# A transformer block on one Trainium2 core: two tiles of x turned by DMA rather than by TensorE, and low parts computed amid the attention steps

## The chip, the core and the metric

The kernel runs on one core of one Trainium2 chip. The metric is the time of one execution in device microseconds; lower is better. Matrix products run on TensorE (PE in the profile), elementwise work on VectorE (DVE), ScalarE (ACT) and GpSimd (POOL), and nearly all DMAs are issued from the queue of SyncE (SP), which issues them in the order of the program.

## What is computed

One layer for S = 2048 rows of D = 512, with 32 heads of 16: a layer norm without weights, a product with wqkv, attention of each row to itself and seven earlier rows at a distance of 2, a product with wo, the residual; then a second norm, a product with w1 (512 x 1792), a squared ReLU, a product with w2, and the residual. Cut to what matters:

```python
q, k, v = (layernorm(x) @ wqkv) as 3 x 32 heads x 2048 x 16
idx = s - [0, 2, .. 14]
logits = (q[s] . k[idx]) / 4, masked where idx < 0
o = softmax(logits) weighted v[idx]
h = x + o @ wo
out = h + relu(layernorm(h) @ w1 + b1) ** 2 @ w2 + b2
```

## The kernel before

The 2048 rows are 16 tiles of 128 rows (rows a stride apart, so that the rows a window reaches lie in the same partition). All operands are f32. A product is made as three products of split operands: each operand is rounded to a **high part** (`xh`, `oh`: a ScalarE copy, L147, `hi`) and a **low part**, the rest (`xl`, `ol`: a VectorE subtraction, L150, `lo`), and `mm3` (L222) adds high x high, low x high and high x low, four matmuls each. The left operand has to be turned (rows to columns) first: `transposes` (L202) does it by four TensorE matmuls with the identity (L205) into a PSUM bank, from which the two parts are read.

A second way to turn is there for tiles of o (the attention's output) and of h: `turn_split` (L591) copies the tile on ScalarE into two planes of 16 bits (L594), `turn_dma` (L596) turns all eight 128x128 blocks of the planes by one DMA in SP's queue (L598), `turn_join` (L601) puts the halves together again on ScalarE (L603), and the high and low part follow as above. It uses no TensorE.

**Order of the work.** The program is written as a row of slots, one for each product or half product of TensorE. `end_slot(pe)` closes one: it runs the chores due (`at`), then `pump()`, then the late chores (`after`). `pump` (L417) issues attention steps: each is an operation of VectorE (the product of q and k, L343; sums over the head, L377; the mask, L386; maximum and difference, L394 and L396; the sum, L366, and its reciprocal; the weights, L371; the product with v, L354), with the exponential on ScalarE (L400) and sums on GpSimd (L411). It issues as many steps as keep a model clock of VectorE (`now["dve"]`) level with that of TensorE (`now["pe"]`).

**The stages.** In the first 16 slots (n = 0 to 15, loop at L951) TensorE makes q, k and v of tiles 0 to 3 by four groups of head pairs, `qkv(t, gp)` with t = n % 4. Then `first_phase(t0)` (L980) for t0 = 4, 6, ... 14 makes those of two tiles at a time, in twelve half products. Each result is copied out of its bank by ScalarE (`evac`, L501) into one of two halves of the buffer `y2`, in turn, and once a pair of tiles is there, `store` issues the DMAs (L480, L483) to `qkv_d` in DRAM. Four PSUM banks go round, so a product needs the evacuation of the product four before it, and an evacuation needs the store that last read its half of `y2`. `store_halo` (L470) copies a piece of what was stored, and so waits for that store. Attention loads k, q and v windows back (L251 for k and v, L264 for q); q is copied to PSUM by ScalarE (L272). Later come the products with wo (`wo_product`, L658; `h_add`, L637, adds the residual and starts the statistics of h) and the two products of the MLP.

For tiles 4 and 5 of x, the statistics (`x_stats`) are due in slots 8 and 9, the norm (L200) in slots 11 and 12, and `x_T` in slots 13 and 14: TensorE turns the tile, ScalarE makes the high part in that slot, VectorE the low part behind that slot's attention steps. The first product that needs tile 4 is the one behind slot 15. Tiles 6 and 7 are normed in half products 6 and 7 of `first_phase(4)` and turned in half products 9 and 11.

Of the kernel before, what the change touches and what calls it, by code (L numbers as in the profile page):

```python
# [9 lines left out]
F32R = mybir.dt.float32r  # L10
# [6 lines left out]
P = 128  # L17
KB = D // P
FB = F // P
R = 4  # L20
RI = 2
# [7 lines left out]
NEG = -4.0e9  # L29
ROWS = 15  # L30
LAG = 3
AS = (4, 5, 8, 9, 12, 13)
OV = (4, 5, 8, 9, 12, 13)
HV = (4, 5, 8, 9, 12, 13)
SLOW = 1.01, 1.10, 1.06
DELAY = 3
WJ = 2
# [1 line left out]
OT = 4, 5, 10, 12  # L39
WO = 7, 9, 13, 15  # L40
HT = 20, 20, 21, 23
OK = (-6, -2, 4), (-5, -1, 5), (3, 6, 10), (4, 7, 12)
HK = (12, 15, 18), (14, 16, 19)
W2 = (18,)
LH = 3, 4, 10, 11
OP = 6, 7, 12, 13
# [12 lines left out]
def block_kernel(ctx, tc, x, wqkv, wo, w1, b1, w2, b2, out):  # L59
# [42 lines left out]
    def row(name, shape=(P, D), dt=F32):  # L102
        return work.tile(list(shape), dt, name=name, tag="row", bufs=ROWS)
# [3 lines left out]

    due = {}
    late = {}
    now = {"slot": 0, "pe": 0.0, "dve": 0.0, "sub": -1}  # L110

    def at(delta, fn, *a):
        due.setdefault(now["slot"] + delta, []).append((fn, a))

    def after(delta, fn, *a):
        late.setdefault(now["slot"] + delta, []).append((fn, a))

    def end_slot(pe):
        now["pe"] += pe
        run(due)  # L120
        pump()
        run(late)
        now["slot"] += 1

    def run(chores):
        todo = chores.get(now["slot"], [])
        while todo:
            fn, a = todo.pop(0)
            fn(*a)
# [83 lines left out]
    def hi_T(tr, h_dst):  # L213
        for d, src in parts(tr, h_dst):
            hi(d, src)
# [201 lines left out]
    def pump(until=None):  # L417

        while (done[until] < G) if until is not None else (now["dve"] < now["pe"]):
            todo = sums[:]  # L420
            sums.clear()
            t = next(stream, "end")
            for a in todo:
                add_up(*a)
            if t == "end":
                now["dve"] = 1e9
                return
            if t is None:
                now["dve"] = max(now["dve"], now["pe"])
                return  # L430
            dve(t * SLOW[min(now['sub'] + 1, 2)])


    xt, xT = {}, {}
# [16 lines left out]
    def x_T(t):  # L451
        tr = transposes(xt.pop(t))
        xT[t] = row("xh", (P, KB, P), F32R), row("xl", (P, KB, P), F32R)
        at(0, hi_T, tr, [xT[t][0]])
        after(0, lo_T, tr, [xT[t][0]], [xT[t][1]])
# [104 lines left out]
    oT = {}  # L560
# [9 lines left out]
    def o_T(t):  # L570
        s, j = divmod(t, RI)
        pump(until=s)
        tr = transposes(o_t[s][:, j, :])
        if t % R == RI:

            ohl = att.tile([P, 2, KB, P], F32R, name="ohl", tag="o", bufs=3)
            oT[t] = ohl[:, 0], ohl[:, 1]
        else:
            oT[t] = row("oh", (P, KB, P), F32R), row("ol", (P, KB, P), F32R)
        at(0, hi_T, tr, [oT[t][0]])  # L580
        at(0, lo_T, tr, [oT[t][0]], [oT[t][1]])

    planes = {}
# [7 lines left out]
    def turn_split(key, src):  # L591

        planes[key] = src, row("pl")
        nc.scalar.copy(two_planes(planes[key][1]), halves_of(src))  # L594

    def turn_dma(key):  # L596
        src, pl = planes[key]
        nc.sync.dma_start_transpose(  # L598
            src.bitcast(U16).rearrange("p (n c) -> p n c", c=P), pl.bitcast(U16))

    def turn_join(key):  # L601
        src, pl = planes[key]
        nc.scalar.copy(halves_of(pl).rearrange("p two n -> p n two"),  # L603
                       two_planes(src).rearrange("p two n -> p n two"))
        planes[key] = pl.rearrange("p (k c) -> p k c", k=KB)
# [6 lines left out]
    def o_join(t):  # L612
        turn_join(("o", t))
        tr = planes.pop(("o", t))
        if t % R == RI:
            ohl = att.tile([P, 2, KB, P], F32R, name="ohl", tag="o", bufs=3)
            oT[t] = ohl[:, 0], ohl[:, 1]
        else:
            oT[t] = row("oh", (P, KB, P), F32R), row("ol", (P, KB, P), F32R)
        hi_T(tr, [oT[t][0]])  # L620
        after(0, lo_T, tr, [oT[t][0]], [oT[t][1]])

    def h_split(t):
        turn_split(("h", t), hn.pop(t))
# [12 lines left out]
    def h_add(t, ps):  # L637
        h = hs[t]
        nc.vector.tensor_tensor(out=h, in0=ps, in1=h, op=ALU.add)
        dve(0.7)  # L640
        (act_stats if t in AS else norm_stats)(t, h)

    def h_norm(t):
        hn[t] = row("hn")
# [306 lines left out]
    for n in range(16):  # L951
        gp, t = divmod(n, 4)
        qkv(t, gp, (lambda: start_T(t + 1)) if n < 3 else None)
        if n < 2:
            x_norm(n + 2)
        if n == 0:
            x_stats(3)
        if n < 6:
            for k in (0, 1):
                at(0, hi_wqkv, n // 2 + 1, n % 2 * 2 + k)  # L960
                after(0, lo_wqkv, n // 2 + 1, n % 2 * 2 + k,
                      nc.gpsimd if k or n < 2 else nc.vector)
        if n == 1:
            load_wqkv(3)
        if n == 13:
            consts()
        if n in (5, 6, 12, 14):
            at(0, load_x, n - 1 if n < 7 else n // 2)
        if n in (8, 9):
            at(0, x_stats, n - 4)  # L970
        if n in (11, 12):
            at(0, x_norm, n - 7)
        if n in (13, 14):
            x_T(n - 9)
        end_slot(2.09)


# [2 lines left out]
    def first_phase(t0):  # L980
        def chores(m):
            if t0 + 3 < 16:
                if m in (0, 2):
                    at(0, x_stats, t0 + 2 + m // 2)

                early = t0 == 12
                if m + early in (6, 7):
                    at(0, x_norm, t0 - 4 + m + early)
                if m in XT[early]:
                    x_T(t0 + 2 + XT[early].index(m))  # L990
            if t0 + 5 < 16 and m in (6, 9):
                at(0, load_x, t0 + 2 + m // 3)
            if jobs and m % 3 == 0:
                at(0, weight_job)
            k = t0 // 2 * 12 - 72 + m
            if k == 19:
                dve(HOLD)
            for t in range(R):
                if k == OT[t]:
                    at(0, load_h, t)  # L1000
                    if t not in OV:
                        o_T(t)
                if t in OV and k in OK[t]:
                    at(0, (o_split, lambda t: turn_dma(("o", t)), o_join)[OK[t].index(k)], t)
                if t in HV and k in HK[t]:
                    at(0, (h_split, lambda t: turn_dma(("h", t)),
                           lambda t: turn_join(("h", t)))[HK[t].index(k)], t)
                if k == WO[t]:
                    wo_product(t, (1, 3, 4, 6))
                    now["pe"] += 2.73  # L1010
                if k == HT[t]:
                    (at(0, h_parts, t) if t in HV else h_T(t))
            if k in W2:
                at(0, load_w2, W2.index(k))

        def half(m):
            end_slot(1.37)
            chores(m)

        for n in range(6):  # L1020
            chores(2 * n)
            qkv_of(t0 + n % 2, n // 2, lambda: half(2 * n + 1))
            end_slot(1.37)
# [41 lines left out]
    for u in range(R - 1):  # L1065
# [11 lines left out]
        for i in js:  # L1077
            t = R * (u + 1) + i
            if not end:
                a = i // 2 if u == 2 else 0  # L1080
                o0 = OP[i] - a
                if t in OV:
                    turned = [(o0, at, 0, o_split, t), (o0, after, 0, turn_dma, ("o", t)),
                              (o0 + 2, at, 0, o_join, t)]
                else:
                    turned = [(o0, o_T, t)]
                if t in HV:
                    h0 = 12
                    turned += [(h0, at, 0, h_split, t), (h0, after, 0, turn_dma, ("h", t)),
                               (h0 + 2, at, 0, turn_join, ("h", t))]  # L1090
                for p, *what in ((LH[i] - a, at, 0, load_h, t), *turned,
                                 (WP[i] - a, wo_product, t, (0, 1, 2 + 3 * a, 3 + 3 * a))):
                    todo.setdefault(p, []).append(what)
                p, h = (HP[i], i % 2) if u < 2 else HL[i]
                if t in HV:
                    todo.setdefault(p, []).append((at, 0, h_parts, t))
                else:
                    (todo, halves)[h].setdefault(p, []).append((h_T, t))
            todo.setdefault(UP[i], []).append((at, 0, unspill, R * u + i))
# [10 lines left out]

        for p in range(FB + LAG):
            more = 0.0
# [76 lines left out]
    h = hs[S // P - 1]  # L1189
# [34 lines left out]
```

## Time and profile before

| | us |
|---|---|
| runs of the kernel before, median (lowest to highest) | 512.49 (512.13 to 514.7) |
| the profiled execution's own time | 512.31 |
| its span in the profile | 510.5 |
| TensorE busy | 501.9 |
| VectorE, GpSimd, ScalarE busy | 376.7, 351.2, 290.9 |
| granted TensorE clock, mean | 0.999 of full speed |

The profile shows one execution. A row of a timeline gives start and length in us, engine, line, operation, the tiles written and read with their shapes, how many instructions were merged into the row (x4), and in brackets the idle time before it and what ended that. A row of the waits gives the waiting operation, what it waited for, the total in us, how often, and the longest. A row of a group gives the shortest, median and longest of its instructions in ns and when the first and last of them ran. Rows of SPq are DMAs as SP's queue issues them.

### The profile page before, as it was taken

The page shows a single profiled execution, that of the slowest core. Times are in us where ns is not written, and L with a number is a line of the kernel's source. Part 1 is how long each engine was busy: PE and PEld are TensorE (multiplying, and loading weights), DVE is VectorE, ACT ScalarE, POOL GpSimd, SP SyncE. Part 2 cuts the span into 40 slices and gives each one's busy share as a digit, 9 for nine tenths or more (in the row PEclk, how much of TensorE's full clock was granted, in tenths as well). Part 3 has the DMA queues.
Part 4 walks back from the last instruction along what each step waited for, and adds up shares of the span by engine and source line. Part 5 has one row for each costly group of instructions (what it writes and reads, how often), then busy time and mean ns, then how long its engine had stood idle before and what let it go on. Part 6 is the DMA issues. An engine that isn't in the chain of part 4 may idle for free. (4 is left out here: it accounts for less than half of the span.)

```text
span 510.5 us, 7598 instructions
## 1 busy us (share of the span) xinstructions
PE 501.9 (98%) x2460; PEld 424.4 (83%) x2460; DVE 376.7 (74%) x512; ACT 290.9 (57%) x552; POOL 351.2 (69%) x430
## 2 busy tenths in 40 slices
PE   7999999999999999999999999999999999999997
PEld 6999788888888888888888878888888888998986
DVE  5479899988998899788879979899963046832233
ACT  4634686767434767485364557264564737666541
POOL 4714799895786798786778768776897364685610
PEclk9999999999999999999999999999999999999999
DMA  8678998989677889666587955767672172444112
GB/s 264 180 225 203 256 295 299 271 285 274 204 225 214 276 301 272 200 199 174 182 253 217 226 166 163 202 199 249 207 152 67 52 217 84 160 142 133 62 42 83
DMA packets 100912, 100.52 MB, mean 197 GB/s; under 512 B 21000, under 2 KB 69384, under 8 KB 100872
## 3 DMA queue, kind: packets, MB, share of 16 engines
q1 hardware_dynamic: 99928, 99.52, 65.4%
q10 hardware_dynamic: 944, 0.52, 0.3%
q8 instruction: 19, 0.31, 0.3%
q14 instruction: 21, 0.17, 0.1%
HBM read 72.65 MB, written 24.25 MB: 190 GB/s over the span
## 5 line engine op out<-in xcount | busy, mean ns | idle before, releaser
L411 POOL TENSOR_TENSOR pr<-pr 128x512 f32<-128x512 f32 (+1 forms) x128 | 132.5, 1035 | 45.7 <-DVE pr L354 40.3
L232 PE MATMUL mm<-big_l,w_h 128*128 128x512 f32 x336 | 88.7, 390 | 0.0
L354 DVE TENSOR_TENSOR pr<-ex,v 128x1024 f32<-128x1024 f32 x64 | 78.2, 1222 | 12.8 <-POOL o L411 6.5
L343 DVE TENSOR_TENSOR pr<-qp,k 128x1024 f32<-128x1024 f32 x64 | 76.9, 1202 | 5.6 <-ACT qp L272 5.5
L377 DVE TENSOR_REDUCE ex<-pr 128x64 f32<-128x1024 f32 x64 | 78.4, 1226 | 1.9
L232 PEld LDWEIGHTS mm<-big_l,w_h 128*128 128x128 f32 x336 | 62.8, 188 | 13.0
L150 POOL TENSOR_TENSOR rl<-r,rh 128x512 fp32r<-128x512 f32 x42 | 56.2, 1339 | 19.6 <-ACT rh L147 16.5
L232 PE MATMUL mm<-big_h,xl 128*128 128x512 f32 (+1 forms) x208 | 56.0, 379 | 0.2 <-DVE xl L150 0.2
L232 PE MATMUL mm<-big_h,xh 128*128 128x512 f32 (+1 forms) x208 | 53.5, 378 | 0.7 <-ACT xh L147 0.7
L232 PE MATMUL mm<-big_l,xh 128*128 128x512 f32 (+1 forms) x208 | 52.8, 375 | 0.0
L870 PE MATMUL acc<-big_l,rh 128*128 128x512 f32 x190 | 52.2, 390 | 0.0
L870 PE MATMUL acc<-big_h,rh 128*128 128x512 f32 x190 | 52.1, 391 | 0.0
L501 ACT COPY y<-mm 128x512 f32<-128x512 f32 (+1 forms) x52 | 28.6, 552 | 41.2 <-PE mm L232 33.0
L870 PE MATMUL acc<-big_h,rl 128*128 128x512 f32 x190 | 51.7, 389 | 0.0
L846 ACT ACTIVATE r<-mm,b_sb 128x512 f32<-128x512 f32 x42 | 28.8, 685 | 32.4 <-PE mm L232 32.3
L232 PE MATMUL mm<-big_l,w_l 128*128 128x512 f32 x168 | 45.0, 389 | 0.0
L232 PEld LDWEIGHTS mm<-big_h,xh 128*128 128x128 f32 x208 | 37.6, 188 | 7.0 <-ACT xh L147 1.5
L232 PEld LDWEIGHTS mm<-big_l,xh 128*128 128x128 f32 x208 | 38.2, 188 | 6.1 <-POOL big_l L150 0.2
L232 PEld LDWEIGHTS mm<-big_h,xl 128*128 128x128 f32 x208 | 37.2, 188 | 5.8 <-DVE xl L150 0.6
L870 PEld LDWEIGHTS acc<-big_h,rl 128*128 128x128 f32 x190 | 35.7, 188 | 7.5
L870 PEld LDWEIGHTS acc<-big_l,rh 128*128 128x128 f32 x190 | 35.5, 188 | 7.4
L870 PEld LDWEIGHTS acc<-big_h,rh 128*128 128x128 f32 x190 | 34.9, 188 | 6.7
(160 smaller groups left out, 904.1 us busy)
## 6 DMA issues: line engine op xcount, KB each, us to landing
k<-qkv_d SPq DMA_DIRECT2D x48, 288.0 KB, 2.8
v<-qkv_d SPq DMA_DIRECT2D x48, 288.0 KB, 3.2
qkv_d<-y SPq DMA_DIRECT2D x18, 512.0 KB, 4.2
big_l<-w2l_d SPq DMA_DIRECT2D x24, 256.0 KB, 3.0
xt<-in_A_x_dram SPq DMA_DIRECT2D x16, 256.0 KB, 4.6
q<-qkv_d SPq DMA_DIRECT2D x32, 128.0 KB, 4.7
h<-in_A_x_dram SPq DMA_DIRECT2D x16, 256.0 KB, 3.9
h_d<-h SPq DMA_DIRECT2D x16, 256.0 KB, 3.2
```

The lines of the kernel that those rows point to most:

```text
L150: eng.tensor_tensor(out=dst, in0=src, in1=h, op=ALU.subtract)
L232: nc.tensor.matmul(ps, l(k), r(k), start=(n == 0), stop=(n == 3 * KB - 1))
L343: nc.vector.tensor_tensor(out=pr.rearrange("p i w h d -> p i w (h d)"), in0=qps["now"][:, j % 2].unsqueeze(2).to_broadcast([P, RI, W, GC]) ...
L354: nc.vector.tensor_tensor(out=p2, in1=vwin, op=ALU.mult, in0=e1[:, :, :, j * GH:(j + 1) * GH].unsqueeze(4).to_broadcast([P, RI, W, GH, DH]))
L377: nc.vector.tensor_reduce(out=lf[:, :, :, j * GH:(j + 1) * GH], in_=pr, axis=X, op=ALU.add)
L411: nc.gpsimd.tensor_tensor(out=dst, in0=p2[:, :, :w], in1=p2[:, :, w:2 * w], op=ALU.add)
L501: nc.scalar.copy(y[:, :, t % RI * GC:(t % RI + 1) * GC], ps[:, :j * GC].rearrange("p (j c) -> p j c", j=j))
L846: nc.scalar.activation(r, ps, AF.Relu, bias=b1_sb[:, f:f + 1])
L870: nc.tensor.matmul(acc[j], l[:, j * P:(j + 1) * P], w[f], start=(first and n < len(js)), stop=(last and n >= len(terms) - len(js)))
```

## The change

Four things change.

- **Tiles 4 and 5 of x** are turned by the second way. Norm in slots 9 and 10 rather than 11 and 12, `x_split` in slots 10 and 11, `turn_dma` late in the same slots, `x_join` with the high part in slots 13 and 14.
- **The norms of tiles 6 and 7** are due in half products 4 and 6 of `first_phase(4)`, not 6 and 7.
- **Low parts of tiles turned by DMA** (4 and 5 of x; 4, 5, 8, 9, 12 and 13 of o) are issued by a new list, `midway`: `pump` runs it amid its steps once VectorE's model clock is within 2.6 of TensorE's, where they came behind all steps of the slot before.
- **The statistics of h** for the same tiles are issued behind the slot's attention steps (`after`) rather than ahead of them.

The tables for the turns of o and h are written more shortly; for the tiles that use them (`OV`, `HV` hold none of tiles 0 to 3) the order of `first_phase` is not touched by that. Cut to its core:

```diff
+HALF = 2.6
...
+    def midway(delta, fn, *a):
+        amid.setdefault(now["slot"] + delta, []).append((fn, a))
     def end_slot(pe):
         now["pe"] += pe
         run(due)
         pump()
+        run(amid)
         run(late)
         now["slot"] += 1
...
         while (done[until] < G) if until is not None else (now["dve"] < now["pe"]):
+            if until is None and now["dve"] > now["pe"] - HALF:
+                run(amid)
             todo = sums[:]
...
         hi_T(tr, [oT[t][0]])
-        after(0, lo_T, tr, [oT[t][0]], [oT[t][1]])
+        (at if t >= 14 else midway)(0, lo_T, tr, [oT[t][0]], [oT[t][1]])
+
+    def x_split(t):
+        turn_split(("x", t), xt.pop(t))
+
+    def x_join(t):
+        turn_join(("x", t))
+        tr = planes.pop(("x", t))
+        xT[t] = row("xh", (P, KB, P), F32R), row("xl", (P, KB, P), F32R)
+        hi_T(tr, [xT[t][0]])
+        midway(0, lo_T, tr, [xT[t][0]], [xT[t][1]])
...
-        (act_stats if t in AS else norm_stats)(t, h)
+        if t in AS:
+            after(0, act_stats, t, h)
+        else:
+            norm_stats(t, h)
...
-        if n in (11, 12):
-            at(0, x_norm, n - 7)
+        if n in (9, 10):
+            at(0, x_norm, n - 5)
+        if n in (10, 11):
+            at(0, x_split, n - 6)
+            after(0, turn_dma, ("x", n - 6))
         if n in (13, 14):
-            x_T(n - 9)
+            at(0, x_join, n - 9)
...
-                if m + early in (6, 7):
-                    at(0, x_norm, t0 - 4 + m + early)
+                if m + early in ((4, 6) if t0 == R else (6, 7)):
+                    at(0, x_norm, t0 - 4 + m + early if t0 > R else t0 + m // 2)
```

**ScalarE, slots 9 to 14.** Lines of the changed kernel are some numbers higher: L200 is L205, L272 L277, L501 L508, L147 L152, L594 L601, L603 L610. `xt` are the tiles of x (358 is tile 4, 376 tile 5), `y2` the evacuations, `qp` the copy of q, `pl` the planes. Before:

```order
L501 COPY y2_90<-mm_402 128x6x64
L501 COPY y2_90<-mm_430 128x6x64
L272 COPY qp_469<-q_399 128x256
L400 ACTIVATE ex_226<-ex_226 128x128
L501 COPY y2_90<-mm_453 128x6x64
L200 ACTIVATE xt_358<-xt_358,rs_420 128x512
L501 COPY y2_90<-mm_484 128x6x64
L200 ACTIVATE xt_376<-xt_376,rs_446 128x512
L501 COPY y2_90<-mm_501 128x6x64
L147 CAST xh_550<-tr_545 128x512
```

And in the changed kernel:

```order
L508 COPY y2_90<-mm_402 128x6x64
L205 ACTIVATE xt_358<-xt_358,rs_420 128x512
L508 COPY y2_90<-mm_430 128x6x64
L205 ACTIVATE xt_376<-xt_376,rs_446 128x512
L601 COPY pl_469<-xt_358 128x1024
L277 COPY qp_473<-q_399 128x256
L405 ACTIVATE ex_226<-ex_226 128x128
L508 COPY y2_90<-mm_454 128x6x64
L601 COPY pl_503<-xt_376 128x1024
L508 COPY y2_90<-mm_489 128x6x64
L508 COPY y2_90<-mm_508 128x6x64
L610 COPY pl_469<-xt_358 128x1024
```

Both norms and the first split now stand ahead of the copy of q.

**SP's queue, the same slots.** Rows from the load of q that follows, in the changed kernel; before, the halo copies (there L470) come right behind the load of q:

```order
L269 DMA q<-qkv_d 128x2x128
L605 DMA_TRANSPOSE xt<-pl 128x8x128 x2
L477 DMA qkv_d<-qkv_d 2x8x64 x2
L447 DMA xt<-in_A_x_dram 128x512
L487 DMA qkv_d<-y_90 128x3x128 x2
L256 DMA k<-qkv_d 128x704
```

The two turns stand behind the loads of k and q and ahead of the halo copies, a load of x and a store.

**VectorE, around tiles 8 and 9 of o** (near 290 to 305 us of the profile before). `ol` is the low part, `h` the residual added to the product with wo. Before:

```order
L343 TENSOR_TENSOR pr<-qp,k 128x1024
L371 TENSOR_TENSOR ex<-ex,sm 128x256
L354 TENSOR_TENSOR pr<-ex,v 128x1024
L377 TENSOR_REDUCE ex<-pr 128x16x4
L343 TENSOR_TENSOR pr<-qp,k 128x1024
L150 TENSOR_TENSOR ol<-pl,oh 128x512
L639 TENSOR_TENSOR h<-wo,h 128x512
```

And in the changed kernel, where L150 is L155 and L639 is L656:

```order
L348 TENSOR_TENSOR pr<-qp,k 128x1024
L155 TENSOR_TENSOR ol<-pl,oh 128x512
L376 TENSOR_TENSOR ex<-ex,sm 128x256
L359 TENSOR_TENSOR pr<-ex,v 128x1024
L382 TENSOR_REDUCE ex<-pr 128x16x4
L656 TENSOR_TENSOR h<-wo,h 128x512
L348 TENSOR_TENSOR pr<-qp,k 128x1024
```

The low part moved ahead of four attention steps, and one of these (L348) is now behind the residual.

More of the change, by code (lines that the diff above doesn't have):

```diff
@@ L31 @@
 LAG = 3
+HALF = 2.6
 AS = (4, 5, 8, 9, 12, 13)
-OV = (4, 5, 8, 9, 12, 13)
-HV = (4, 5, 8, 9, 12, 13)
+OV = (4,5,8,9,12,13)
+HV = (4,5,8,9,12,13)
 SLOW = 1.01, 1.10, 1.06
@@ L41 @@
 HT = 20, 20, 21, 23
-OK = (-6, -2, 4), (-5, -1, 5), (3, 6, 10), (4, 7, 12)
-HK = (12, 15, 18), (14, 16, 19)
+HK = (12, 18), (14, 19)
 W2 = (18,)
@@ L109, in block_kernel @@
     late = {}
+    amid = {}
     now = {"slot": 0, "pe": 0.0, "dve": 0.0, "sub": -1}
@@ L1000, in chores @@
                     at(0, load_h, t)
[L1001 to L1007, printed above, removed]
+                    o_T(t)
+                if t in HV and k == HK[t][0]:
+                    at(0, h_split, t)
+                    after(0, turn_dma, ("h", t))
+                if t in HV and k == HK[t][1]:
+                    at(0, turn_join, ("h", t))
                 if k == WO[t]:
@@ L1080, in block_kernel @@
                 a = i // 2 if u == 2 else 0
-                o0 = OP[i] - a
+                o0 = OP[i] - a - (2 if i >= RI and t in OV else 0)
                 if t in OV:
-                    turned = [(o0, at, 0, o_split, t), (o0, after, 0, turn_dma, ("o", t)),
+                    turned = [(o0, at, 0, o_split, t), (o0, at if i >= RI else after, i // RI, turn_dma, ("o", t)),
                               (o0 + 2, at, 0, o_join, t)]
```

## The prediction

> **What bounds the kernel now.** I read the page's busy shares first, then TensorE's waits, then its timeline around the two places that the change touches.
>
> ```profile
> span 510.5 us, 7598 instructions
> PE 501.9 (98%) x2460; PEld 424.4 (83%) x2460; DVE 376.7 (74%) x512; ACT 290.9 (57%) x552; POOL 351.2 (69%) x430
> ...
> PE tr L918 <- POOL mhalf L904: 1.3, 1, 1.3
> PE tr L205 <- DVE xt L196: 1.3, 1, 1.3
> PE wo L232 <- DVE ol L150: 1.2, 2, 0.6
> PE mm L232 <- ACT xh L147: 0.7, 1, 0.7
> PE tr L205 <- ACT xt L200: 0.4, 1, 0.4
> PE mm L232 <- DVE xl L150: 0.2, 1, 0.2
> ```
>
> TensorE is busy for 98% of the span, and all its waits together (the third number is the total, then the count, then the longest) come to about 5 us. So TensorE is the bound from end to end, and the sum has two sides only: what TensorE no longer does or no longer waits for, and what it newly waits for. The other engines count only where TensorE comes to wait for them. The span is 510.5 us, this execution's own time 512.31 us and the median of the runs 512.49 us; I sum on 512.31 and add the 0.18 at the end.
>
> **Part one, what goes away.** Tiles 4 and 5 are no longer turned on TensorE.
>
> ```profile
> 35.47 0.85 PE L232 MATMUL mm<-big_h,xh 128*128 128x384 f32 x4
> ...
> 37.55 0.85 PE L232 MATMUL mm<-big_h,xh 128*128 128x384 f32 x4
> ...
> 39.63 0.60 PE L205 MATMUL tr<-ident,xt 128*128 128x128 f32 x4
> ...
> 42.16 0.60 PE L205 MATMUL tr<-ident,xt 128*128 128x128 f32 x4
> ...
> 44.70 1.08 PE L232 MATMUL mm<-big_h,xh 128*128 128x512 f32 x4
> ```
>
> Product 13 starts at 37.55 and tile 4's first product, number 16, at 44.70. A product of this stage without a turn takes 2.08 us (product 12 starts at 35.47). So 7.15 us hold three products, 6.24 us, and two turns, **0.91 us**. That goes for certain, and number 16 would start at 43.79 if its operand were there.
>
> Three waits can go as well.
>
> ```profile
> 57.59 0.66 PE L205 MATMUL tr<-ident,xt 128*128 128x128 f32 x4 [0.44 <-ACT xt L200]
> ...
> 63.94 1.19 PE L232 MATMUL mm<-big_h,xl 128*128 128x512 f32 x4 [0.17 <-DVE xl L150]
> ...
> 295.86 1.20 PE L232 MATMUL wo<-wo_h,ol 128*128 128x512 f32 x4 [0.61 <-DVE ol L150]
> ...
> 304.88 1.21 PE L232 MATMUL wo<-wo_h,ol 128*128 128x512 f32 x4 [0.56 <-DVE ol L150]
> ```
>
> The norm of tile 6 is issued two half-products earlier, so the 0.44 goes. The two waits for low parts of o, 0.61 and 0.56, are on an instruction that the change takes out from behind attention steps:
>
> ```profile
> 290.25 0.62 ACT L147 CAST oh<-pl 128x512 fp32r<-128x512 f32 x1
> ...
> 294.82 0.97 DVE L150 TENSOR_TENSOR ol<-pl,oh 128x512 fp32r<-128x512 f32 x1
> ```
>
> Its operand is there at 290.87, and it runs at 294.82, behind four steps. In the new order it stands right behind the first of these, so it can run near 291 and be done some 3 us earlier than now: both waits go, 1.17 us. What it displaces are attention steps, which nothing on TensorE waits for in this stage: no row of the waits names one. The 0.17 of tile 6's low part I count as gone and price its successor below. Sum of part one: 0.91 + 0.44 + 1.17 + 0.17 = **2.69 us**, which alone gives 509.62.
>
> **Part two, when tile 4 arrives.** The turn becomes a chain: norm, split into planes (ScalarE), DMA, join, high part (ScalarE). The links by the rows of before, where the same helpers turn o:
>
> ```profile
> L594 ACT COPY pl<-o x6: 1037/1040/1042, 187.2 to 372.5; 128x1024 uint16<-128x1024 uint16 x6
> L603 ACT COPY pl<-o x6: 1160/1170/1175, 198.1 to 383.8; 128x1024 uint16<-128x1024 uint16 x6
> L598 SPq DMA_TRANSPOSE o<-pl x6: 1237/1270/1632, 192.9 to 380.0; - x6
> ...
> DMA to landing us min/median/max: 4.3/4.7/5.1
> ```
>
> And what stands around it at this place:
>
> ```profile
> 33.11 0.86 ACT L501 COPY y<-mm 128x384 f32<-128x384 f32 x2 [5.23 <-DMA qkv_d<-y]
> 33.86 0.40 ACT L272 COPY qp<-q 128x256 f32<-128x256 f32 x1
> ...
> 36.86 0.82 ACT L200 ACTIVATE xt<-xt,rs 128x512 f32<-128x512 f32 x1
> ...
> 42.79 0.59 ACT L147 CAST xh<-tr 128x512 fp32r<-128x512 f32 x1
> ...
> 35.10 0.26 POOL L168 TENSOR_SCALAR rs<-mv,rs 128x1 f32<-128x1 f32 x1
> ...
> 36.05 1.21 DVE L343 TENSOR_TENSOR pr<-qp,k 128x1024 f32<-128x1024 f32 x1
> ...
> 37.30 0.33 SPq L251 DMA_DIRECT2D k<-qkv_d  x1
> 37.68 0.43 SPq L264 DMA_DIRECT2D q<-qkv_d  x1
> 38.20 1.23 SPq L470 DMA_DIRECT2D qkv_d<-qkv_d  x2
> ```
>
> The two evacuations at 33.11 wait for a store that the change does not touch. Between them ScalarE now has tile 4's norm, so they end near 34.7. Tile 5's norm needs its scale from GpSimd at 35.36 and takes 0.82: to 36.2. The split of tile 4 follows, 1.04: to 37.2. Only then comes the copy of q, before at 33.86: to 37.6. VectorE's product on that copy, before at 36.05, now starts at 37.6 and ends at 38.8. The load of k, before issued at 37.30 just as that product was over, overwrites k and so waits for it: 38.85, and q behind it, to 39.65. Behind these two in the same queue stands the turn of tile 4: issued at 39.65, landed 4.7 later at 44.35; join 1.17 and high part 0.59: **46.1**. TensorE would be ready at 43.79. Stall **2.3 us** (1.9 with the shortest landing, 2.7 with the longest). If the k load waited for nothing, the DMA would still wait for the split: 38.0, so 44.5 and a stall of 0.7; that is the lower bound. Tile 5, 1.25 us behind in the queue, has its high part near 48.3, and TensorE reaches it at 46.1 + 2.75 = 48.85: no wait.
>
> The Trainium skill, page "VectorE: DVE Perf Modes", section "The three transpose paths", puts a 128x128 block of 16 bits at 390 ns on TensorE and 1309 ns by DMA, and its "Rules for kernel authors" choose TensorE wherever a PSUM destination will do; that speaks against this edit. A tile is eight such blocks in two planes of four, an estimate from that page of 10.5 us, and the stall would be 5.8 us longer. The trace's 4.3 to 5.1 us for all eight says otherwise, and I go by the trace.
>
> **Part three, what the late chain pushes.** VectorE has tile 4's low part in line behind its step at 41.4, and waits there for the high part, from 43.0 to 46.1. With tile 5's part behind it, the step that stood at 45.77 comes at about 51.05, 5.3 us late.
>
> ```profile
> 45.77 1.22 DVE L343 TENSOR_TENSOR pr<-qp,k 128x1024 f32<-128x1024 f32 x1
> ...
> 57.73 0.29 DVE L366 TENSOR_REDUCE sm<-ex 128x16 f32<-128x128 f32 x1 [2.01 <-ACT ex L400]
> ...
> 63.20 0.68 DVE L150 TENSOR_TENSOR xl<-tr,xh 128x512 fp32r<-128x512 f32 x1
> ```
>
> At 57.73 it had 2.01 us of idle time; this takes 2 us of the lateness, if ScalarE is not late itself. Then 3.3 us are left at 63.20, where tile 6's low part already came 0.17 too late for TensorE. The new order puts that part one step earlier (1.23 less): 63.20 + 0.68 - 1.23 + 3.3 is 66.0. TensorE is later by 2.3 - 0.91 - 0.44 = 0.95 there, and wants it at 63.77 + 0.95 = 64.7. A stall of 1.3; none if VectorE catches up 2 us more, 3.3 if ScalarE's share in the idle time is late too. I take **1.6**, near the first, and 0.2 for tile 7, whose part keeps its place. After that TensorE has itself become later by 2.8 and VectorE's remaining lateness is small beside it.
>
> SP's queue is pushed too:
>
> ```profile
> 45.41 0.91 SPq L480 DMA_DIRECT2D qkv_d<-y  x2
> ...
> 49.86 1.24 SPq L470 DMA_DIRECT2D qkv_d<-qkv_d  x2
> ```
>
> Two issues of 1.25 and the 1.5 that k is late put every store behind by 4 us: that of 45.41 to 49.4, landed (4.4 by the halo copy that follows it at 49.86) by 54. That frees the buffer for tile 4's first evacuation, whose bank TensorE wants back four products on, 46.1 + 4 x 2.75 = 57.1. Three microseconds are left, so I cost this at nothing; the rival below prices it without that cover. ScalarE has 2 x (1.04 + 1.17) more and no row of waits on it in this stage beyond those priced. The statistics of h moved behind the attention steps cost nothing, as no wait of TensorE's names a norm of h.
>
> Sum: 509.62 + 2.3 + 1.6 + 0.2 = 513.7, and 513.9 beside the median.
>
> **The rivals.** *VectorE catches up* (20%): the stall at tile 4 stays, that at tile 6 doesn't appear, because the idle time at 57.73 and slots with fewer steps take all 5.3. For it speaks that 2 of 5.3 are seen to be absorbed; against it that the steps between have no other idle time. 509.62 + 2.3 = 511.9, so 512.1. *No new stall* (10%): tile 4 lands before 43.8, since the copy of q or the k load turns out not to hold the queue; against it stand the 37.30 and 37.68 rows, which follow the product at 36.05 at once. With the lower bound 0.7 left or none it is 509.8 to 510.5. *SP holds the evacuations* (17%), the one that ends slower: the stores behind the two turns land later than 57.1, TensorE waits for a bank, and every store after it is late by the same. The row at 33.11 shows that such a wait exists, 5.23 us of ScalarE's. It decides from 3 us more lateness of SP than I count, and costs what is beyond; with 2 to 4 us on top of the forecast, 515.9 to 517.9. *Twice as long turns* as by the page (2%): 519.7. If the waits at 295 and 304 should stay, each case is 1.17 longer.
>
> **How the numbers follow.** The forecast, 513.9, gets 51%; its own bounds are 512.4 (stall 1.9, tile 6 at 0.5) and 515.6 (3.3 at tile 6). The range takes in the second case and most of the bank rival: 510.7 to 516.8. A measurement of this kernel tells about 0.5% from no change, here below 509.93 or above 515.05. Faster takes most of the third case, 0.1; slower takes the bank rival, the page's and a fifth of the forecast's own, 0.32; the rest, 0.58, is within.
>
> **What would show it.** In the new profile the gap on TensorE in front of the first product 512 wide, at 44 to 46, with a high part on ScalarE as its releaser: over 1.9 if the chain is right, below 0.7 if the queue did not hold. The issue of the first turn should stand near 39.7, behind q. A wait for a low part near 65 decides between the forecast and its first rival, waits of TensorE for evacuations between 55 and 70 show the bank rival, and the waits for ol at 295 and 304 should be gone. The prediction is wrong if the scale of tile 5 or the two evacuations at 33 come elsewhere than I hold, as all of part two hangs on 33.97 and 35.36.

## The result and the profile after

The changed kernel takes 517.66 us (median of 4 runs, 517.51 to 518.3), the kernel before 512.74 in the same comparison: a ratio of 1.0105, 95% interval 1.0087 to 1.0123. It is slower by about 5 us; 513.9 was forecast, with 516.8 as the upper end.

The page's busy shares of the changed kernel and its waits of TensorE, in the columns used before (total, count, longest):

```profile
span 515.6 us, 7571 instructions
PE 503.7 (98%) x2452; PEld 424.5 (82%) x2452; DVE 375.9 (73%) x512; ACT 294.9 (57%) x556; POOL 350.8 (68%) x430
...
PE mm L237 <- ACT xh L152: 4.5, 3, 2.4
PE tr L938 <- POOL mhalf L924: 1.3, 1, 1.3
PE mm L237 <- ACT r L866: 1.0, 1, 1.0
PE mm L237 <- DVE xl L155: 0.6, 2, 0.4
PE mm L237 <- DVE ol L155: 0.4, 1, 0.4
PE wo L237 <- DVE ol L155: 0.2, 1, 0.2
```

TensorE's order of work is the same in both kernels but for eight transposes, so its timeline can be laid beside that of before, product by product. The difference of the starts says where time was won or lost; it stays the same between the places named here. First the rows of the changed kernel at the places where it changes:

```profile
43.06 0.86 PE L237 MATMUL mm<-big_l,xh 128*128 128x384 f32 x4
45.38 1.19 PE L237 MATMUL mm<-big_h,xh 128*128 128x512 f32 x4 [1.47 <-ACT xh L152]
...
58.03 0.66 PE L210 MATMUL tr<-ident,xt 128*128 128x128 f32 x4
...
65.79 1.21 PE L237 MATMUL mm<-big_h,xh 128*128 128x512 f32 x4 [2.40 <-ACT xh L152]
...
88.45 1.20 PE L237 MATMUL mm<-big_h,xl 128*128 128x512 f32 x4 [0.35 <-DVE xl L155]
...
231.95 1.21 PE L237 MATMUL mm<-big_l,w_h 128*128 128x512 f32 x4 [0.98 <-ACT r L866]
...
241.36 1.20 PE L237 MATMUL mm<-big_l,w_h 128*128 128x512 f32 x4 [0.42 <-DVE ol L155]
...
301.38 1.07 PE L237 MATMUL wo<-wo_h,ol 128*128 128x512 f32 x4
...
309.54 1.07 PE L237 MATMUL wo<-wo_h,ol 128*128 128x512 f32 x4
...
390.76 1.19 PE L237 MATMUL wo<-wo_h,ol 128*128 128x512 f32 x4 [0.22 <-DVE ol L155]
```

And the same products before, as far as the prediction has not shown them (44.01, 84.08, 226.23, 235.00 and 385.84):

```profile
44.01 0.85 PE L232 MATMUL mm<-big_l,xh 128*128 128x384 f32 x4
...
84.08 1.07 PE L232 MATMUL mm<-big_h,xl 128*128 128x512 f32 x4
...
226.23 1.17 PE L232 MATMUL mm<-big_l,w_h 128*128 128x512 f32 x4
...
235.00 1.07 PE L232 MATMUL mm<-big_l,w_h 128*128 128x512 f32 x4
...
385.84 1.07 PE L232 MATMUL wo<-wo_h,ol 128*128 128x512 f32 x4
```

| place | changed kernel against before there, us | what happened |
|---|---|---|
| end of slot 15 | -0.95 | the two turns are gone |
| tile 4's first product | +0.68 | waits 1.47 for its high part |
| turn of tile 6 | +0.44 | the wait of 0.44 is gone |
| tile 6's first product | +3.11 | waits 2.40 for its high part |
| tile 9 | +4.37 | waits for low parts |
| 232 | +5.72 | waits 0.98 for r |
| 241 | +6.36 | waits 0.42 for a low part of o |
| 301 and 310 | +5.52, +4.66 | both waits for ol are gone |
| 391 to the end | +4.92, +5.03 | waits 0.22 |

The gains came as forecast. The losses are four groups (tile 4, tile 6, tiles 7 to 9, and 232 to 241), of which the forecast had one and a half.

### The profile page after: what moved, and what is told of

Read it like the earlier page. It is cut to its first block, busy times and chain, and to the rows that moved or that the text cites. A ratio compares the mean times of both kernels' runs of the same rounds, so it can differ in the third digit from the quotient of the medians.

```text
span 515.6 us, 7571 instructions
## 1 busy us (share of the span) xinstructions
PE 503.7 (98%) x2452; PEld 424.5 (82%) x2452; DVE 375.9 (73%) x512; ACT 294.9 (57%) x556; POOL 350.8 (68%) x430
## 5 line engine op out<-in xcount | busy, mean ns | idle before, releaser
L416 POOL TENSOR_TENSOR pr<-pr 128x512 f32<-128x512 f32 (+1 forms) x128 | 135.0, 1055 | 52.8 <-DVE pr L359 47.3
L348 DVE TENSOR_TENSOR pr<-qp,k 128x1024 f32<-128x1024 f32 x64 | 76.8, 1200 | 14.8 <-ACT qp L277 9.5
L155 POOL TENSOR_TENSOR rl<-r,rh 128x512 fp32r<-128x512 f32 x42 | 54.3, 1294 | 16.7 <-ACT rh L152 16.7
L508 ACT COPY y<-mm 128x512 f32<-128x512 f32 (+1 forms) x52 | 28.6, 552 | 31.9 <-PE mm L237 20.3
```

The source lines that it names most:

```text
L155: eng.tensor_tensor(out=dst, in0=src, in1=h, op=ALU.subtract)
L348: nc.vector.tensor_tensor(out=pr.rearrange("p i w h d -> p i w (h d)"), in0=qps["now"][:, j % 2].unsqueeze(2).to_broadcast([P, RI, W, GC]) ...
L416: nc.gpsimd.tensor_tensor(out=dst, in0=p2[:, :, :w], in1=p2[:, :, w:2 * w], op=ALU.add)
L508: nc.scalar.copy(y[:, :, t % RI * GC:(t % RI + 1) * GC], ps[:, :j * GC].rearrange("p (j c) -> p j c", j=j))
```

## The experiments

Theory at the start: the late turn of tiles 4 and 5 costs what stands ahead of 100 us, and the waits near 232 and 241 come from the later part of the change by itself, the statistics of h queued behind the attention steps. Rival: all of it is lateness that starts at tile 4 and is carried on. All ratios below are to the kernel before on the same chip, with their 95% intervals; the edits are to the changed kernel, but for `e12`.

**Both tiles of x back on TensorE** (`e1`, and once more as `e16`). The rest of the change stays.

```diff
-        if n in (9, 10):
-            at(0, x_norm, n - 5)
-        if n in (10, 11):
-            at(0, x_split, n - 6)
-            after(0, turn_dma, ("x", n - 6))
+        if n in (11, 12):
+            at(0, x_norm, n - 7)
         if n in (13, 14):
-            at(0, x_join, n - 9)
+            x_T(n - 9)
...
-                if m + early in ((4, 6) if t0 == R else (6, 7)):
-                    at(0, x_norm, t0 - 4 + m + early if t0 > R else t0 + m // 2)
+                if m + early in (6, 7):
+                    at(0, x_norm, t0 - 4 + m + early)
```

> The changed kernel with tiles 4 and 5 of x turned by TensorE again and the norms of tiles 4 to 7 where they were; the low parts of o amid the steps and the later statistics of h stay. By TensorE's starts, the changed kernel is 0.95 us ahead at slot 16, then loses 1.6 at tile 4, 2.6 at tile 6, 0.3 at tile 7, 0.9 at tiles 8 and 9, then 1.2 and 0.6 near 230 to 241 us, wins 1.5 at 295 and 304 and loses 0.4 near 390. Theory (x chain and later part are separate): only what stands behind 220 us is left, 1.8 + 0.4 - 1.5, so 0.7 above before, about 513.3. Rival (the losses near 230 are lateness carried on from tiles 4 to 9): they go too, and 1.5 is won: about 511.1.

Measured: 509.97 us, 0.9954 (0.9937 to 0.9971), faster than both kernels. The waits near 232 and 241 are gone with the turn, though the later statistics and the low parts amid the steps are still there:

```profile
PE tr L210 <- DVE xt L201: 1.2, 1, 1.2
PE mm L237 <- ACT xh L152: 0.7, 1, 0.7
PE mm L237 <- DVE xl L155: 0.2, 1, 0.2
```

The rival is right: the turn by DMA, with the earlier norms that this edit takes back as well, is behind all the losses, 7.7 us of them (517.66 - 509.97). No run separates the norms of tiles 6 and 7 from the turn.

**Only the turn by DMA** (`e2`): the kernel before with tiles 4 and 5 turned by DMA, norms earlier.

```diff
-        (at if t >= 14 else midway)(0, lo_T, tr, [oT[t][0]], [oT[t][1]])
+        after(0, lo_T, tr, [oT[t][0]], [oT[t][1]])
...
-        midway(0, lo_T, tr, [xT[t][0]], [xT[t][1]])
+        after(0, lo_T, tr, [xT[t][0]], [xT[t][1]])
...
-        if t in AS:
-            after(0, act_stats, t, h)
-        else:
-            norm_stats(t, h)
+        (act_stats if t in AS else norm_stats)(t, h)
```

> The kernel before with only tiles 4 and 5 of x turned by DMA and the earlier norms; low parts behind the steps, statistics of h ahead of them. Theory (separate): -0.95 - 0.35 + 1.6 + 2.6 + 0.3 + 0.9, so 4.1 above before, about 516.7, and no new wait near 230. Rival (carried on): the 1.8 near 230 is there too, and the 1.2 of waits for ol at 295 and 304 stays: about 518.5.

Measured: 522.68 us, 1.0203 (1.0177 to 1.0229), slower than either had it. There is no wait near 232, but one of 3.75 us for a low part of o at 312, where before has 0.56. VectorE stands there behind a copy of q:

```profile
304.32 1.22 DVE L348 TENSOR_TENSOR pr<-qp,k 128x1024 f32<-128x1024 f32 x1 [2.20 <-ACT qp L277]
```

ScalarE makes that copy behind the statistics of h, as in `e8` below, so the wait is not carried lateness alone; how it divides is not shown. About 1.6 us more are TensorE's clock behind this wait (last section).

**The statistics, and the low parts of o** (`e3`: the first edit undone; `e4`: the second).

```diff
-        if t in AS:
-            after(0, act_stats, t, h)
-        else:
-            norm_stats(t, h)
+        (act_stats if t in AS else norm_stats)(t, h)
```

> The changed kernel with the statistics of h ahead of the slot's attention steps again. Theory (the 0.98 wait for r near 231 and the 0.42 behind it come from statistics queued on ScalarE behind an exponential that waits 6.4 us for VectorE): 1.8 less than the changed kernel, about 515.9. Rival (they come from the low parts amid the steps, or are lateness carried on): no change, 517.6.

Measured: 518.09 us, 1.0118 (1.0088 to 1.0148), with waits of 0.80 at 220, 0.48 for r at 233 and 0.45 at 242. The order of the statistics is not the cause of those waits.

```diff
-        (at if t >= 14 else midway)(0, lo_T, tr, [oT[t][0]], [oT[t][1]])
+        after(0, lo_T, tr, [oT[t][0]], [oT[t][1]])
```

> The changed kernel with the low parts of o behind the steps again (those of x stay amid). Theory (low parts amid the steps only take away the two waits at 295 and 304): 1.5 slower than the changed kernel, about 519.1. Rival (they also cause the waits near 231 and 241, by pushing attention steps back): 1.5 - 1.8, about 517.3, and the wait for r near 231 is gone.

Measured: 518.58 us, 1.0122 (1.0091 to 1.0153). The wait for r near 232 is gone, and waits of 1.47 at 309 and 1.44 at 391 for low parts of o stand in its place. Each theory had half of it: where the lateness shows depends on what is queued, while the time of the three kernels hardly differs.

**Giving VectorE fewer steps** (`e5`): its model clock 2.5 ahead from slot 14 on.

```diff
+        if n == 14:
+            dve(2.5)
         end_slot(2.09)
```

> The changed kernel with VectorE's model clock put 2.5 ahead behind slot 14, so that from there on about two attention steps fewer are issued ahead of any low part; nothing else. Theory (after the late tiles 4 and 5 VectorE stays 1.5 to 2.5 us late against TensorE for two hundred us, because nothing in the order gives the time back, and each wait for a low part or for r from tile 7 on is that lateness): the waits from 85 to 245 us are gone, 0.9 + 1.8, and those at tile 6 shrink: about 4 us above before or less, some 1 to 3 below the changed kernel. Rival (the waits near 85 and 231 have causes of their own, ScalarE's order or the low parts amid the steps): within 0.5 us of the changed kernel, 5 above before.

Measured: 518.04 us, 1.0117 (1.0098 to 1.0135). The wait at tile 6 falls from 2.40 to 0.96, with 0.47 for its low part behind it, and there is none at tiles 8 and 9; but near 231 and 241 it is 1.25 and 1.01, and a new one for r, 1.03, stands at 323. The steps not made early are made later.

**Two slots earlier** (`e6`): load, statistics, norm, split and turn; the join stays.

```diff
-        if n in (5, 6, 12, 14):
-            at(0, load_x, n - 1 if n < 7 else n // 2)
-        if n in (8, 9):
-            at(0, x_stats, n - 4)
-        if n in (9, 10):
-            at(0, x_norm, n - 5)
-        if n in (10, 11):
-            at(0, x_split, n - 6)
-            after(0, turn_dma, ("x", n - 6))
+        if n in (3, 4, 12, 14):
+            at(0, load_x, n + 1 if n < 7 else n // 2)
+        if n in (6, 7):
+            at(0, x_stats, n - 2)
+        if n in (7, 8):
+            at(0, x_norm, n - 3)
+        if n in (8, 9):
+            at(0, x_split, n - 4)
+            after(0, turn_dma, ("x", n - 4))
```

> The changed kernel with load, statistics, norm, split and turn of tiles 4 and 5 of x two slots (4.2 us) earlier; the join stays in slots 13 and 14. Theory (the chain of tile 4 is late by 1.5 to 2 us at slot 16, and all later waits follow from VectorE standing idle for it): no wait for xh at slot 16, VectorE not idle there, no waits from 60 to 245; what is left is before - 0.95 - 0.35 - 1.5, about 2.5 to 3 below before, 509.5. Rival (two turns and four copies more in the queues of SP and ScalarE cost time wherever they stand): the wait at slot 16 goes, those at 60 to 245 us stay, about 3 above before.

Measured: 515.29 us, 1.0055 (1.0039 to 1.0072). The wait at slot 16 falls to 0.39 and nothing waits near 232: so far the theory. But at tile 6 there are still 2.20 for the high part and 1.20 for the low part. SP's queue is still late (the halo copies at 52.18, before 49.86). These waits are those of an execution of 512.98 us, 2.3 below the median of the ten, so they do not account for all of the median's loss.

**Tile 5 alone by DMA** (`e7`).

```diff
-        if n in (10, 11):
+        if n == 11:
             at(0, x_split, n - 6)
             after(0, turn_dma, ("x", n - 6))
-        if n in (13, 14):
+        if n == 13:
+            x_T(n - 9)
+        if n == 14:
             at(0, x_join, n - 9)
```

> The changed kernel with tile 4 turned by TensorE (norm early, turn in slot 13) and only tile 5 by DMA. One turn, one split, one join less, and tile 5 is needed 2.7 us later than tile 4. Theory (lateness of the chain alone counts): tile 5's high part comes before 46.5 and nothing waits; the time is that of the kernel with both on TensorE less one turn, 0.45: about 2.5 below before, 509.5. Rival (SP's and ScalarE's queues are pushed by any such turn): half of the 7.6 us between the changed kernel and the one with both tiles on TensorE remains, about 1.5 above before.

Measured: 514.28 us, 1.0045 (1.0028 to 1.0062). Tile 5 itself is not waited for, and yet tile 6's high part is, by 2.39 us, as with two turns (in an execution of 516.26 us, 2.0 above the median). The rival holds: one turn does it. What ScalarE does there in the changed kernel:

```profile
64.14 0.62 ACT L152 CAST wo_h<-raw 128x512 fp32r<-128x512 f32 x1 [2.68 <-DMA raw<-in_A_wo_dram]
64.67 0.58 ACT L508 COPY y<-mm 128x512 f32<-128x512 f32 x1
65.15 0.59 ACT L152 CAST xh<-tr 128x512 fp32r<-128x512 f32 x1
```

Tile 6's high part (`xh`) stands behind the split of a piece of wo, whose load stands in SP's queue behind the halo copies:

```profile
38.25 0.33 SPq L256 DMA_DIRECT2D k<-qkv_d  x1
38.63 1.81 SPq L269 DMA_DIRECT2D q<-qkv_d  x1
40.54 2.71 SPq L605 DMA_TRANSPOSE xt<-pl  x2
...
50.41 0.91 SPq L487 DMA_DIRECT2D qkv_d<-y  x2
...
53.84 1.71 SPq L477 DMA_DIRECT2D qkv_d<-qkv_d  x2
...
57.82 0.46 SPq L558 DMA_DIRECT2D raw<-in_A_wo_dram  x1
```

The halo copies come at 53.84 instead of 49.86, and so the second piece of wo is issued at 57.82 and split at 64.14. Before, the order is the same:

```profile
53.70 0.46 SPq L551 DMA_DIRECT2D raw<-in_A_wo_dram  x1
...
59.74 0.63 ACT L147 CAST wo_h<-raw 128x512 fp32r<-128x512 f32 x1 [1.31 <-DMA raw<-in_A_wo_dram]
...
60.74 0.59 ACT L147 CAST xh<-tr 128x512 fp32r<-128x512 f32 x1
...
62.68 1.09 PE L232 MATMUL mm<-big_h,xh 128*128 128x512 f32 x4
```

ScalarE waited for this load there too, and the high part was done at 61.33, 1.35 us ahead of TensorE. It is now 4.41 later (65.15), and 4.41 - 1.35 = 3.06 is TensorE's lateness at tile 6 (3.11).

**The split of wo later** (`e9`), and with the earlier chain (`e10`: the edits of `e6` and this one).

```diff
-        at(5, split)
+        at(7 if len(jobs) >= 16 else 5, split)
```

> The changed kernel with the split of the four pieces of wo due seven half products after their load, not five, so that tile 6's high part no longer stands behind the second piece on ScalarE. Theory (SP's queue is 4 us late, the second piece lands at 64.1, and ScalarE waits for it ahead of tile 6's high part): the wait of 2.4 us at tile 6 is gone; what VectorE's own lateness leaves for tile 6's low part is 0.5 to 1.5, so 1 to 2 us less than the changed kernel, 516. Rival (the high part would be as late without it, since evacuations or norms hold ScalarE): still 2 us or more at tile 6, 517.6.

> The chain of tiles 4 and 5 two slots earlier and the later split of wo, both at once. Theory (these two are where the turn by DMA costs its time): of the waits at slot 16 (0.4 left when only earlier), tile 6's high part (2.2) and low part (1.2) only up to 1 in all is left, and with 0.95 + 0.35 + 1.5 won the time is 1 to 2 below before, at the level of the kernel with both tiles on TensorE or up to 1 above it. Rival (some other cost of the turns): 2 or more above before.

Measured: `e9` 520.48 us, 1.0161 (1.0144 to 1.0179); `e10` 514.89, 1.0051 (1.0034 to 1.0068). In `e9` the wait for the high part is gone, and TensorE waits 1.40 for tile 6's low part and 1.28 at tile 8 instead; in `e10` it waits 3.06 for tile 6's low part, which comes 1.81 later than before (65.01, not 63.20), while TensorE comes 1.10 earlier (61.58, not 62.68). So two chains end at tile 6 (in the changed kernel the high part is done at 65.74, the low part at 66.63), and to take one away shows the other. The expected gain was not there: `e9` is slower than the changed kernel, and `e10` no faster than `e6`.

**The copy of q first** (`e11`).

```diff
-            at(0, x_split, n - 6)
+            after(0, x_split, n - 6)
```

> The changed kernel with each split behind its slot's attention steps, so that the copy of q stands ahead of tile 4's split on ScalarE. Theory (the copy of q behind the split is 1 us of the lateness of SP's queue and of VectorE; the rest is the norms ahead of it and the turns): k is loaded 1 us earlier, the turn itself not earlier, since the split is; the wait at slot 16 stays at 1.5 to 2, that at tile 6 is 0.5 to 1 less: 517. Rival (the copy of q sets when the turn is issued): the wait at slot 16 falls to 0.7 or less and all later ones with it, 515 or below.

Measured: 518.65 us, 1.0132 (1.0116 to 1.0147). The load of k is issued at 37.59, not 38.25, and the wait at slot 16 is 1.88: the copy of q did not set when the turn landed. The wait at tile 6 is 0.70, but its product starts at 65.78, as in the changed kernel (65.79).

**VectorE out of the line** (`e13`, with the later split of wo `e14`, with the earlier chain as well `e15`): the low parts of tiles 4 and 5 on GpSimd.

```diff
-        midway(0, lo_T, tr, [xT[t][0]], [xT[t][1]])
+        lo(nc.gpsimd, xT[t][1], tr, xT[t][0])
```

> The changed kernel with the low parts of tiles 4 and 5 of x on GpSimd, so that VectorE doesn't stand in line for the high parts (3.0 and 0.3 us idle) nor compute them (1.3 us). Theory (what costs time behind tile 4 is that VectorE's row of attention steps lost 5 us there and TensorE has to follow it from tile 6 on): the steps at 48 to 57 us are 1 to 2 us later than before and not 4 to 5, no wait for a low part from tile 6 to 9 and none near 230 to 241; ScalarE's wait for the piece of wo stays, so 513 to 515. Rival (the 4 us of SP's queue set it all): steps as late as in the changed kernel, 517 to 518.

> The same with the split of wo two half products later. The later split alone moved the wait at tile 6 from the high part to the low part and won nothing. Theory (VectorE's lateness stood behind it): now the wait at tile 6 goes altogether, 511.5 to 513. Rival (a third thing holds tile 6): 2 us at tile 6 stay.

> The same with the chain of tiles 4 and 5 two slots earlier as well. Theory: no wait above 0.5 behind slot 16, 0.95 + 0.35 + 1.5 won, about 509.5 to 510.5, level with the kernel with both tiles on TensorE. Rival: GpSimd, now in line for the high parts, holds the sums and with them VectorE's buffers: 512 or more.

Measured: `e13` 516.71 us, 1.0098 (1.0081 to 1.0115); `e14` 515.82, 1.008 (1.0059 to 1.0102); `e15` 514.47, 1.0061 (1.0041 to 1.008). The waits of `e13`:

```profile
PE mm L237 <- ACT xh L152: 4.8, 4, 1.6
...
PE mm L237 <- DVE big_l L155: 0.7, 1, 0.7
PE tr L210 <- DVE xt L201: 0.3, 1, 0.3
PE mm L237 <- POOL xl L155: 0.2, 1, 0.2
```

No low part of x or o made by VectorE and no r is waited for any more (the 0.7 is for a low part of a weight, at 346.89). Near 232 and 241 TensorE is 4.77 us behind the kernel before, not 5.72 and 6.36, and waits for nothing: those waits were VectorE's lateness. At tiles 8 and 9 the run shows less, since TensorE itself comes there later (4.80 behind, not 4.37). Left are the high parts, which ScalarE makes: 1.63 at tile 4, 0.91 at tile 6 and 1.43 at tile 7. As a remedy it gave next to nothing (the intervals overlap), since VectorE then waits elsewhere (1.82 us for a copy of q at 47.92). In `e14` the wait at tile 6 does not go altogether: 1.59 for its low part is left, so the theory missed there. In `e15`, GpSimd's low part holds TensorE by 0.82 and tile 7's high part by 1.33; the rival was nearer. None of these versions beats the kernel before.

**What the gain needs** (`e8`: `e1` with the statistics of h ahead, so the low parts of o alone; `e12`: the later statistics alone). `e8` has the edit of `e3` on top of `e1`; `e12` has its reverse on the kernel before.

> Both tiles of x turned by TensorE, norms as before, statistics of h ahead of the steps as before: of the change only the low parts of o amid the steps are left. Theory (the later statistics do nothing by themselves): the same as with them, 2 below before, 510. Rival (they are what frees ScalarE or VectorE): 1 us slower than that, 511.

> The kernel before with only the later statistics of h. With both tiles on TensorE the low parts amid the steps alone gave no gain, the same with later statistics 2 us. Theory (the two work together: the low parts of tiles 8 and 9 come early only if ScalarE's high parts and VectorE's steps are not behind the statistics): alone it gives nothing or a loss, 512 to 513. Rival (the later statistics are the gain): 510.

> The kernel with both tiles of x on TensorE, low parts of o amid the steps and later statistics, once more, beside the others on one chip. It was 2 us below before (0.9954, 0.9937 to 0.9971). Theory (a real gain, the two waits of 0.6 at 295 and 304 and what else came with them): 0.995 to 0.997 again. Rival (scatter of that chip): within 0.2% of before.

Measured: `e8` 512.10 us, 1.0007 (0.9992 to 1.0023); `e12` 512.06, 1.0 (0.9989 to 1.0011); both together, `e16`, 510.35, 0.9974 (0.9962 to 0.9985). My theory for `e8` fell: the later statistics, nothing by themselves, are needed. The row of VectorE that shows why, in `e8`:

```profile
299.05 1.22 DVE L348 TENSOR_TENSOR pr<-qp,k 128x1024 f32<-128x1024 f32 x1 [2.20 <-ACT qp L277]
...
303.70 0.96 DVE L155 TENSOR_TENSOR ol<-pl,oh 128x512 fp32r<-128x512 f32 x1
```

With the statistics ahead, ScalarE copies q only behind them, at 298.65, VectorE waits 2.20 for that copy, and tile 9's low part comes at 303.70, too late by 1.35 for TensorE. In `e1` the copy is at 294.88 and the low part at 300.90, in time.

## Why the prediction was wrong

- **What goes away** was right. Forecast 0.91, 0.44 and 1.17; measured by the table's differences 0.95, 0.24 and 0.84 + 0.86 (the last two with TensorE's restart behind each wait). That the gain at 304 hung on the later statistics too, which I had costed at nothing, was not seen.
- **Tile 4's chain** was right up to the queue: the copy of q behind the split, the load of k behind the product on it (38.25, forecast 38.85), the turns behind the load of q. The last two links were both off, and it is luck that they nearly cancel. The load of q took 1.81 us of the queue instead of 0.43, so the turn was issued at 40.54 (forecast 39.65); and it landed within 3.0 us, as its join shows, not in 4.7:

```profile
43.52 1.16 ACT L610 COPY pl<-xt 128x1024 uint16<-128x1024 uint16 x1 [4.33 <-DMA xt<-pl]
```

  The high part was done at 45.34 (46.1), and the stall was 1.47, or 1.6 with the restart, against 2.3. The case of twice as long turns is out. Where the issue of the first turn moved, its landing did not follow: issued at 38.49 (`e11`) it was joined at 44.01, issued at 41.01 (`e9`) at 44.05. What sets the landing is not shown.
- **The step that failed is part three.** Its lateness of VectorE was near (4.30 us, forecast 5.3), but it said of the 2.01 us of idle time at 57.73, "this takes 2 us of the lateness". It took 0.3:

```profile
54.28 1.23 DVE L359 TENSOR_TENSOR pr<-ex,v 128x1024 f32<-128x1024 f32 x1
...
60.60 1.22 DVE L348 TENSOR_TENSOR pr<-qp,k 128x1024 f32<-128x1024 f32 x1 [1.71 <-ACT y L508]
...
64.81 1.23 DVE L359 TENSOR_TENSOR pr<-ex,v 128x1024 f32<-128x1024 f32 x1
...
75.62 1.22 DVE L359 TENSOR_TENSOR pr<-ex,v 128x1024 f32<-128x1024 f32 x1 [0.64 <-POOL o L416]
...
81.77 1.23 DVE L348 TENSOR_TENSOR pr<-qp,k 128x1024 f32<-128x1024 f32 x1 [1.53 <-POOL o L416]
86.57 1.23 DVE L359 TENSOR_TENSOR pr<-ex,v 128x1024 f32<-128x1024 f32 x1
```

  These are VectorE's rows in the changed kernel. The products with v of 54.28, 64.81 and 86.57 stand before at 49.98, 60.81 and 79.92: the lateness is 4.30, then 4.00, then 6.65. The engine it waits for was late too, so the idle time moved along, and waits for GpSimd came on top. What had looked like slack was a wait whose releaser hung on the same cause.
- **"I cost this at nothing"**, on SP's queue, failed as well. The 4 us of lateness were right (53.84 against 49.86), their price was not: I looked at the evacuations' bank and missed the load of wo behind the halo copies, which ScalarE awaits ahead of tile 6's high part, in the kernel before too. So TensorE stalls at tile 6 for the high part, 2.67 us by the table (3.11 - 0.44), and not 1.6 for the low part. `e7` shows that wait of 2.39 us even where tile 5 alone is turned by DMA and nothing waits for tile 5.
- **"After that ... VectorE's remaining lateness is small"** failed: 6.65 us against TensorE's 3.11 at tile 6 leaves 3.5, and TensorE lost 1.26 from tile 7 to 9 (4.37 - 3.11) and, 140 us later, 1.35 and 0.64 near 232 and 241, all by the table: 3.2 us. The waits at tiles 8 and 9 are for VectorE's own low parts, and `e13` shows that those near 232 and 241 are VectorE's too.
- In the sum, the losses were put at 4.1 us (2.3, 1.6 and 0.2) and came to 7.8: 1.63 at tile 4, 2.67 at tile 6, then the 3.2 above and 0.26 near 391.
- The rival "SP holds the evacuations" gave nearly the right time, in part by luck: the queue was right and the instruction wrong, and of its 2 to 4 us on top of the forecast only 1.1 (2.67 for 1.6) came that way. The rest is mostly VectorE's lateness.

One thing in these runs looks like a puzzle. `e3`, `e4`, `e5` and `e11` wait much less for tile 6's high part than the changed kernel, and are no faster:

| | clock, 44 to 48 and 48 to 52 us | tile 6's high part starts | the product on it starts | TensorE's wait ahead of it, us |
|---|---|---|---|---|
| changed kernel | 1.00, 1.00 | 65.15 | 65.79 | 2.40 |
| `e3` | 0.77, 0.81 | 65.22 | 65.86 | 0.71 |
| `e4` | 0.90, 0.68 | 64.63 | 65.27 | 0.30 |
| `e5` | 1.00, 1.00 | 64.31 | 64.95 | 0.96 |
| `e11` | 0.86, 0.72 | 65.14 | 65.78 | 0.70 |

The high part comes within 0.9 us in all of them, and TensorE goes on 0.64 behind its start. In `e3`, `e4` and `e11` TensorE only comes to it later, having run at a lower clock behind the wait at tile 4; in `e5` the high part is 0.84 earlier. So the length of this wait says little, and the time at which the operand comes says what it costs.

What stays open: what sets the landing of the turns, what the earlier norms of tiles 6 and 7 do by themselves, and how much of `e2`'s wait at 312 is carried lateness.

## What to carry to other kernels

An engine that is busy for three quarters of the span can still have no spare time in a stage: lateness put on it there is not worked off, only handed on, until the order of the work gives it a hole of its own. Before counting an idle stretch as cover, ask whether its releaser hangs on the thing that is late. And of a transfer put into an ordered queue, follow every load behind it to the instruction that awaits it, not only the stores. When two runs are compared, compare when an operand comes, not how long the wait for it is.

## What the runs showed of the hardware

TensorE's granted clock fell behind some of the waits. The stretches of `e10`, of which the column ahead of the last two is the clock, and its products there:

```profile
56.00:64.00 8.00, 6.68 (x34) 5.15 (x32) 7.04 (x11) 4.71 (x10) 6.02 (x8) 1.00 1.02 288
64.00:72.00 8.00, 6.26 (x16) 4.92 (x17) 7.90 (x12) 5.68 (x16) 7.44 (x11) 0.57 1.06 364
```

```profile
65.74 2.08 PE L237 MATMUL mm<-big_h,xl 128*128 128x512 f32 x4 [3.06 <-DVE xl L155]
67.62 1.91 PE L237 MATMUL mm<-big_l,xh 128*128 128x512 f32 x4
...
72.19 1.08 PE L237 MATMUL mm<-big_l,xh 128*128 128x512 f32 x4
```

Four matmuls take 1.91 us where they take 1.08 at full clock, for some 6 us behind a wait of 3.06. The same was there behind waits of 1.86 (`e2`, 0.87 and 0.85 in the stretches from 44 to 56 us), 1.84 to 1.97 (`e3`, `e4`, `e9`, `e11`), 1.63 (`e13`, 0.85 and 0.86), 2.39 (`e7`, 0.81 and 0.76 from 64 to 72) and 3.75 (`e2` at 312, 0.65 from 312 to 316). By the starts of the products it cost 1.6 us behind each of the two waits in `e2`, and 2.7 in `e10`, on top of the wait; at tile 4 this only shortens the wait at tile 6. Behind the changed kernel's waits of 1.47 and 2.40, and behind 1.77 in `e5`, the clock stayed at 1.00. The Trainium skill, page "TensorE: Matmul & The Clock Gate", Part 1, puts the half rate behind an idle window of about 3.4 us; here a wait of 1.63 was followed by it in one execution, and one of 2.40 was not in another.
